# Top-k attention and dropless experts on one core: TensorE, ScalarE and VectorE put in a hand-written order by groups of rows

## The chip, the cores and the metric

The kernel runs on one core of one Trainium2 chip. The metric is device time in microseconds (us), the median of three runs. In the profile PE is TensorE's matmul, PEld its weight load, DVE VectorE, ACT ScalarE, POOL GpSimd and SP the engine that issues most of the DMAs.

## The reference

Two blocks follow each other. Attention has 8 batches, 8 heads, 576 rows, head size 64, and keeps the 32 largest scores of each row:

```
scores = scale * q @ k^T                       # 576 x 576 for each batch and head
kth    = 32nd largest score of each row
attn   = softmax(scores where scores >= kth)   # the rest is masked
x      = attn @ v, heads side by side          # 4608 x 512
logits = x @ w_gate                            # 8 experts
e      = argmax(logits);  gate = softmax(logits)[e]
out    = gate * (relu(x @ w1[e]) @ w2[e])      # w1 512 x 1024, w2 1024 x 512, all float32
```

## The kernel before

**Units, groups, tiles.** Two heads form a unit: 8 batches x 4 units. A unit has nine tiles of 128 rows (four for each head, and one that joins the last 64 rows of both). They are worked on in five groups: four pairs of tiles and a single one. So `work` has 160 groups, 20 for each batch. The loop over `work` (L673 to L710) runs, for group i:

- `search` (L241), on DVE: four rounds of MAX8 (L260) and MATCH_REPLACE8 (L268) over the halves' maxima, one MAX8 over the minima (L265), then `both` (L277) and the threshold `thr` (L281). In its last round it calls `between`, which is `fold` (L233: `hl`, a maximum and a minimum of the two halves of a score row, L237 and L238) for group i+1. On POOL it issues `nbias` (L262), `low` (L283) and `over` (L286).
- `transposed` (L313) for group i-1: for each tile four transposes on PE into a PSUM bank `wTm` (L321), the last 64 columns into `wTl` (L329), and copies to SBUF on ACT (L324 or L326, L332 or L334). Banks named `wTm`, `wTl`, `po`, `px`, `pl` and `rank` share two buffers (`bank`, L192).
- `scores` (L215) for group i+2: eight matmul instructions on PE (L225) into two PSUM tiles `sc` (two buffers), each copied by ACT to `s` (L230).
- `depths` (L291), ACT: `w = relu(low - STEEP * s)` (L295); `weights` (L301): POOL takes `s - w` (L305), ACT the exponential (L308), which also sums the row.
- After a unit's last group, `close` (L613): `outputs` (L336) makes the unit's product with the values on PE (`po`, L350), copies it (`oT`, L351), transposes it (`px`, `pl`, L354 and L357), takes the gate's logits (L360) and copies all of it to SBUF (L355, L364, L366); then the loads of the unit after next are issued on SP. `settle` (L628) follows in steps that `later` (L656) calls in the next groups: `divisors` (L368, DVE), `scaled` (L376, POOL), and after a batch's last unit `route` (L392) and `table` (L462), which choose an expert for each row and write the rows, sorted, to DRAM (`scatter`, L436, an indirect DMA on POOL).
- `pieces` (L594): the expert blocks. A block is 128 sorted rows of one expert: `turned` (L529, transposes `xtp`), 8 pieces of `ph` matmuls (L548), 8 pieces of `py` matmuls (L558), ReLU `hT` and scaling `y` on ACT (L553, L562), and a scatter of the result to `out` on POOL (L563). There are 16 pieces to a block and 40 blocks in the common path. 24 of them are spread over the groups; their number per batch is 0, 4, 4, 5, 4, 5, 4 for the rows of batches 0 to 6, with a new rate taken at the group `FIRST` = 5 of the next batch. Two (`KEEP`) cover the last batch's routing, and 14 (`ALWAYS`) run alone at the end.

**What sets the order.** Except where a dependency is written (`pinned`, L523, keeps an expert's matmul behind the newest score matmul or gate matmul; two `add_manual_dep` in `scaled`), the framework's scheduler orders each engine's queue by its own model of durations. Each engine executes its queue in that order, whatever is ready.

**After the blocks** two tests follow, each with its own branch: rows beyond the 14 blocks (L723), and an exact second pass where `doubt` says that the two-half search may have lost a value (L737). Neither branch is taken here.

Of the kernel before, what the change touches and what calls it, by code (L numbers as in the profile page):

```python
# [43 lines left out]
def kernel(  # L44
# [36 lines left out]
    nc = tc.nc  # L81
# [81 lines left out]
    rest_i = const.tile([1, 1], I32, name="rest_i")  # L163
    done = const.tile([1, E], F32, name="done")
# [13 lines left out]
    def open_pools(st, exact):  # L178
# [10 lines left out]
        k.last_pe = None  # L189
        k.top = 0  # L190

# [3 lines left out]
    def load_unit(b, u):  # L195
        n = SimpleNamespace(u=u)
        qkb = k.load.tile([P, 2, S], F32, name="qkb")
        nc.sync.dma_start(qkb, qk[b, u, :, :, :])
        n.q, n.k = qkb[:, 0, :], qkb[:, 1, :]
        n.v = k.load.tile([P, KC, P], F32, name="vb")  # L200
        nc.sync.dma_start(n.v, v[b, u, :, :].rearrange("(c p) d -> p c d", p=P))
        return n
# [12 lines left out]
    def scores(n, tiles):  # L215
# [6 lines left out]
        for j in range(2):  # L222
            for ps, h, rows, cols in todo:
                d = slice(h * D, (h + 1) * D)
                k.last_pe = nc.tensor.matmul(  # L225
                    ps[rows, j, 0:HF], n.q[d, cols], n.k[d, j * HF:(j + 1) * HF], start=True, stop=True
                ).ins
        s = k.att.tile([P, 2, 2, HF], F32, name="s", bufs=2 if k.exact else 3)
        for m, ps in enumerate(got):
            nc.scalar.copy(s[:, m, :, :], ps[:, :, 0:HF])  # L230
        return s
# [9 lines left out]
    def search(n, tiles, s, hl, between):  # L241
# [14 lines left out]
        for r in range(R):  # L256
# [4 lines left out]
            if r == 0:  # L261
                nc.gpsimd.tensor_scalar_mul(nbias[:, m2], tops[:, m2, 0], -scale)  # L262
                if not k.exact:
                    for m in m_all:
                        nc.vector.max(out=tops[:, m, TOP_K + 1:TOP_K + 9], in_=hl[:, 1, m, :])  # L265
            if r < R - 1:
# [16 lines left out]
        nc.gpsimd.tensor_scalar_mul(low[:, m2], thr[:, m2], STEEP)  # L283
        if not k.exact:
            c = 2 * tiles[0] if len(tiles) == 2 else 2 * NC
            nc.gpsimd.tensor_tensor(  # L286
                n.over[:, c:c + len(tiles)], tops[:, m2, TOP_K + 8], thr[:, m2], op=ALU.subtract
            )
        return low, nbias

    def depths(tiles, s, low):  # L291

        w = k.att.tile([P, 2, S], F32, name="w", bufs=3)
# [7 lines left out]
    def weights(n, tiles, s, w, nbias):  # L301

        c = 2 * tiles[0] if len(tiles) == 2 else 2 * NC
        for m in range(len(tiles)):
            k.last_pool = nc.gpsimd.tensor_tensor(  # L305
                w[:, m, :], s[:, m, :, :].rearrange("p j k -> p (j k)"), w[:, m, :], op=ALU.subtract
            ).ins
            nc.scalar.activation(  # L308
                w[:, m, :], w[:, m, :], AF.Exp, scale=scale, bias=nbias[:, m:m + 1],
                accum_out=n.z[:, c + m:c + m + 1],  # L310
            )
# [24 lines left out]
    def outputs(n, x):  # L336

        oT = oT_of[k.unit % 2]
        k.unit += 1
        for j in range(2):  # L340
            q = slice(j * HF, (j + 1) * HF)
            po = bank("po")
            for c in range(KC):
                for h in range(2):
# [5 lines left out]
                    nc.tensor.matmul(po[r, 0:HF], lhsT, rhs, start=(c == 0), stop=(c == KC - 1))  # L350
            nc.scalar.copy(oT[:, q], po[:, 0:HF])  # L351
# [3 lines left out]
        nc.scalar.copy(x[:, 0:NC, n.u * P:(n.u + 1) * P], px[:, :].rearrange("p (t d) -> p t d", t=NC))  # L355
        pl = bank("pl")
        k.last_pe = nc.tensor.transpose(pl[:, 0:P], oT[:, SM:], ident).ins  # L357
        lw = 2 * E
        for t in range(KC):
            k.last_pe = nc.tensor.matmul(  # L360
                pl[:, P + t * lw:P + (t + 1) * lw], oT[:, t * P:(t + 1) * P],
                wg2[:, n.u, :, :].rearrange("p h e -> p (h e)"), start=True, stop=True,
            ).ins
        nc.scalar.copy(x[:, NC, n.u * P:(n.u + 1) * P], pl[:, 0:P])  # L364
        n.lt = k.small.tile([P, KC, 2, E], F32, name="lt")
        nc.scalar.copy(n.lt, pl[:, P:P + KC * lw].rearrange("p (t h e) -> p t h e", t=KC, h=2))  # L366

# [8 lines left out]
    def scaled(n, x, lg):  # L376

        rzb = rz_of[n.u % 2][:, :].rearrange("p (t h) -> p t h", h=2)
        put = nc.gpsimd.tensor_tensor(n.lt, n.lt, _inner(rzb, E), op=ALU.mult).ins
        if not k.exact:  # L380
            tc.add_manual_dep(put, k.last_pool.name, AFTER)
        if n.u:
            nc.gpsimd.tensor_tensor(lg, lg, n.lt[:, :, 0, :], op=ALU.add)
            nc.gpsimd.tensor_tensor(lg, lg, n.lt[:, :, 1, :], op=ALU.add)
        else:
            nc.gpsimd.tensor_tensor(lg, n.lt[:, :, 0, :], n.lt[:, :, 1, :], op=ALU.add)
        xu = x[:, :, n.u * P:(n.u + 1) * P].rearrange("p t (h d) -> p t h d", h=2)
        put = nc.gpsimd.tensor_tensor(xu, xu, _inner(rzb, D), op=ALU.mult).ins
        if not k.exact:
            tc.add_manual_dep(put, k.last_pool.name, AFTER)  # L390

    def route(x, lg):  # L392
# [11 lines left out]
        nc.vector.tensor_tensor(lg, lg, _inner(mx[:, :], E), op=ALU.subtract)  # L404
        nc.scalar.activation(lg, lg, AF.Exp)
# [4 lines left out]
        nc.tensor.matmul(rp[:, 256:256 + KC * E], ones, ohf, start=True, stop=True)  # L410
        rk = k.small.tile([P, 2, KC * E], F32, name="rk")
# [24 lines left out]
        def scatter(i):  # L436
# [5 lines left out]
            if not k.exact:  # L442
                for other in mine:
# [18 lines left out]
    def table(n, last):  # L462
# [34 lines left out]
        slot_i = sm.tile([1, 2, NSLOT], I32, name="slot_i")  # L497
        nc.vector.tensor_copy(slot_i[:, :, 0:n], slot_f[:, :, 0:n])
        if last:
            nc.vector.tensor_copy(rest_i, upto[:, E - 1:E])  # L500
        else:
# [21 lines left out]
    def pinned(put):  # L523

        if k.last_pe is not None and not k.exact:
            tc.add_manual_dep(put.ins, k.last_pe.name, AFTER)
        return put

    def turned(n):  # L529

        ps = k.ps_m.tile([P, DT, P], F32, name="xtp", tag="m")
        for dt in range(DT):
            pinned(nc.tensor.transpose(ps[:, dt, :], n.x[:, 0, dt * P:(dt + 1) * P], ident))
# [3 lines left out]
    def block(n, following=lambda: None):  # L537
# [5 lines left out]
        for half in range(2):  # L543
            ph = k.ps_m.tile([P, FT // 2, P], F32, name="ph", tag="m")
            for f in range(FT // 2):
                fc = half * (FT // 2) + f
                for dt in range(DT):
                    pinned(nc.tensor.matmul(  # L548
                        ph[:, f, :], n.w1[:, 0, dt, fc * P:(fc + 1) * P], n.xT[:, dt, :],
                        start=(dt == 0), stop=(dt == DT - 1),  # L550
                    ))
                if f == FT // 2 - 1:
# [265 lines left out]
```

## Time and profile before

| | |
|---|---|
| median of 3 runs | 1660.99 us (1656.68 to 1665.58) |
| the profiled execution, its own time | 1664.02 us |
| its span in the trace | 1662.2 us |
| first `thr` (L281) starts | 19.06 us |
| 50th `thr` (group 10 of batch 2) | 421.67 us |
| 160th and last `thr` | 1381.44 us |
| last result scatter issued (L563) | 1648.85 us |

The span is cut by two times in this table. Up to the last `thr` DVE searches one group after the other, and the other engines serve it and fill in pieces of expert blocks; after it PE alone works, on the kept blocks and the 14 last ones. The second row of `thr` matters because up to there hardly any expert block runs. Page 1 of the profile gives busy shares over the whole span, so they mix these stretches; a table of busy time by stretch keeps them apart.

### The profile page before, as it was taken

Reading aid. Unit: us, or ns where it says so; the run is one execution under the profiler, and the core shown is the slowest. Engines: PE = TensorE matmul, PEld = TensorE weight load, DVE = VectorE, ACT = ScalarE, POOL = GpSimd, SP = SyncE. Lnnn points to the kernel's source line nnn. Section 1 sums busy time; section 2 is a strip of 40 time slices with the busy share of each in tenths; the row PEclk is TensorE's granted clock in tenths of the full one; section 3 lists DMA queues with packets and bytes.
Section 4 is the critical chain, followed back from the end, with each engine's and each line's share of the span. In section 5 each row is a group of like instructions: output and inputs, shape, how many; then the busy total and the mean of one; then the engine's idle time right before and its main releaser. Section 6 shows DMA issues by size and latency. Waiting matters only on the chain. (4 is left out here: it accounts for less than half of the span.)

```text
span 1662.2 us, 24985 instructions
## 1 busy us (share of the span) xinstructions
PE 1457.5 (88%) x7874; PEld 924.2 (56%) x7874; DVE 1237.7 (74%) x4258; ACT 934.2 (56%) x1937; POOL 666.3 (40%) x993
## 2 busy tenths in 40 slices
PE   5777878788999989898999999899999987899996
PEld 3444434445555555555666555556655554577764
DVE  8999979999899898889888999977889994000000
ACT  4666646665676676656665777656566763111111
POOL 3444544545444544444345544544345543000000
PEclk8666656668999999989999999989999988999998
DMA  1000010007232533245441633353334333788883
GB/s 59 23 23 23 34 40 23 23 23 266 82 142 78 208 142 120 91 159 202 171 151 54 241 137 136 113 189 136 137 128 160 136 115 143 285 308 304 295 319 130
DMA packets 102191, 230.69 MB, mean 139 GB/s; under 512 B 5150, under 2 KB 25630, under 8 KB 102048
## 3 DMA queue, kind: packets, MB, share of 16 engines
q1 hardware_dynamic: 95904, 210.06, 35.2%
q0 software_dynamic: 6144, 18.92, 3.1%
q8 instruction: 66, 1.08, 0.3%
q14 instruction: 77, 0.63, 0.1%
HBM read 207.68 MB, written 22.33 MB: 138 GB/s over the span
## 5 line engine op out<-in xcount | busy, mean ns | idle before, releaser
L305 POOL TENSOR_TENSOR w<-s,w 128x576 f32<-128x576 f32 x288 | 424.2, 1487 | 302.3 <-ACT w L295 301.8
L260 DVE MAX8 tops<-scr 128x8 f32<-128x288 f32 x864 | 353.8, 445 | 0.9
L225 PE MATMUL sc<-qkb 64*128 64x288 f32 (+1 forms) x1280 | 346.0, 506 | 7.3 <-DMA qkb<-in_qk_dram 5.9
L548 PEld LDWEIGHTS ph<-xTs,w 128*128 128x128 f32 x2560 | 305.3, 198 | 24.2 <-issue 21.9
L548 PE MATMUL ph<-xTs,w 128*128 128x128 f32 x2560 | 315.6, 283 | 1.3 <-ACT xTs L535 1.3
L558 PE MATMUL py<-w,hT 128*128 128x512 f32 x640 | 310.4, 629 | 5.4 <-ACT hT L553 5.3
L308 ACT ACTIVATE w<-w,nbias 128x576 f32<-128x576 f32 x288 | 223.3, 776 | 158.4 <-POOL w L305 156.9
L321 PE MATMUL wTm<-ident,w 128*128 128x128 f32 x1152 | 197.4, 312 | 115.7 <-ACT w L308 113.7
L295 ACT ACTIVATE w<-s,low 128x576 f32<-128x576 f32 x288 | 215.6, 776 | 98.4 <-POOL low L283 98.2
L321 PEld LDWEIGHTS wTm<-ident,w 128*128 128x128 f32 x1152 | 147.8, 158 | 200.5 <-ACT w L308 169.2
L268 DVE MATCH_REPLACE8 scr<-tops,scr 128x288 f32<-128x288 f32 x576 | 250.1, 440 | 0.0
L237 DVE TENSOR_TENSOR hl<-s 128x576 f32<-128x576 f32 (+1 forms) x160 | 130.1, 813 | 129.4 <-ACT s L230 129.0
L225 PEld LDWEIGHTS sc<-qkb 64*128 64x128 f32 (+1 forms) x1280 | 158.4, 204 | 102.6 <-issue 56.7
L558 PEld LDWEIGHTS py<-w,hT 128*128 128x128 f32 x640 | 121.9, 201 | 143.3 <-issue 133.8
L230 ACT COPY s<-sc 128x576 f32<-128x576 f32 x288 | 173.4, 636 | 34.6 <-PE sc L225 25.6
L324 ACT COPY wT<-wTm 128x512 f32<-128x512 f32 x256 | 140.5, 586 | 42.3 <-PE wTm L321 42.2
L350 PE MATMUL po<-wT,vb 128*64 128x288 f32 x1024 | 157.2, 455 | 1.4 <-ACT wT L326 1.4
L563 POOL DMA_INDIRECT out_dram<-y,xg x40 | 40.7, 1017 | 242.3 <-ACT y L562 220.4
L262 POOL TENSOR_SCALAR nbias<-tops 128x2 f32<-128x2 f32 (+1 forms) x160 | 34.9, 218 | 246.4 <-DVE thr L281 139.9
L238 DVE TENSOR_TENSOR hl<-s 128x576 f32<-128x576 f32 (+1 forms) x160 | 129.6, 810 | 0.0
L268 DVE MATCH_REPLACE8 scr<-tops,hl 128x288 f32<-128x288 f32 x288 | 125.3, 440 | 0.1
L260 DVE MAX8 tops<-hl 128x8 f32<-128x288 f32 x288 | 124.8, 441 | 0.0
(119 smaller groups left out, 1244.2 us busy)
## 6 DMA issues: line engine op xcount, KB each, us to landing
w<-in_moe_w_dram SPq DMA_DIRECT2D x80, 2048.0 KB, 11.2
qkb<-in_qk_dram SPq DMA_DIRECT2D x32, 576.0 KB, 3.9
xg<-x_rows SPq DMA_DIRECT2D x40, 257.0 KB, 2.7
vb<-in_v_dram SPq DMA_DIRECT2D x32, 320.0 KB, 3.2
x_rows<-blank SPq DMA_DIRECT2D x9, 257.0 KB, 4.5
x_rows<-x,posi POOLq DMA_INDIRECT x40, 3.0
out_dram<-y,xg POOLq DMA_INDIRECT x40, 2.8
wg<-in_moe_w_gate_dram SPq DMA_DIRECT2D x1, 16.0 KB, 1.9
```

Of the source, the lines that this page charges most:

```text
L225: k.last_pe = nc.tensor.matmul(ps[rows, j, 0:HF], n.q[d, cols], n.k[d, j * HF:(j + 1) * HF], start=True, stop=True).ins
L230: nc.scalar.copy(s[:, m, :, :], ps[:, :, 0:HF])
L260: nc.vector.max(out=tops[:, m, r * 8:(r + 1) * 8], in_=src[m])
L268: nc.vector.match_replace(out=scr[:, m, :], in_to_replace=tops[:, m, r * 8:(r + 1) * 8], in_values=src[m], imm_value=NEG,)
L295: nc.scalar.activation(w[:, m, :], s[:, m, :, :].rearrange("p j k -> p (j k)"), AF.Relu, scale=-STEEP, bias=low[:, m:m + 1],)
L305: k.last_pool = nc.gpsimd.tensor_tensor(w[:, m, :], s[:, m, :, :].rearrange("p j k -> p (j k)"), w[:, m, :], op=ALU.subtract).ins
L308: nc.scalar.activation(w[:, m, :], w[:, m, :], AF.Exp, scale=scale, bias=nbias[:, m:m + 1], accum_out=n.z[:, c + m:c + m + 1],)
L321: nc.tensor.transpose(pm[:, c * P:(c + 1) * P], w[:, m, c * P:(c + 1) * P], ident)
L324: nc.scalar.copy(n.wT[:, :, m, tiles[0] * P:(tiles[0] + 1) * P], pm4)
L350: nc.tensor.matmul(po[r, 0:HF], lhsT, rhs, start=(c == 0), stop=(c == KC - 1))
L548: pinned(nc.tensor.matmul(ph[:, f, :], n.w1[:, 0, dt, fc * P:(fc + 1) * P], n.xT[:, dt, :], start=(dt == 0), stop=(dt == DT - 1),))
L558: pinned(nc.tensor.matmul(py, hT[:, f, :], n.w2[:, 0, f, :], start=(f == 0), stop=(f == FT - 1)))
```

## The change

- **Order.** The loop stands in a `manual_schedule` for PE, ACT and DVE: on these engines the program's order is the queue's order. On POOL the small operations and L305 are put in program order too (`in_turn`), and the indirect DMAs behind the newest L305. `pinned` is gone. SP's order is still the scheduler's.
- **Score products ahead.** `scores` is split into `products` (PE) and copies (ACT). Products are issued four groups ahead, their copies three (`AHEAD`), and the copies stand between the exponentials: copy, exp, copy, exp. `s` has four buffers instead of three.
- **Place of each step.** For group i: search, depths, L305, transposes of group i-1, half of the pieces, copies and exponentials, products of group i+4, the other pieces.
- **Unit ends** run in named places over three groups: first group, both halves of `po` with the products between them and the first `oT` copy, no pieces; second, divisors, second `oT` copy, `px` and `pl`, their copies; third, `logits` and `rows` on POOL, after the first round of the search. A batch's routing follows in the next places, a step each.
- **Pieces** are handed out by tiles (`len(g)`), a group may catch up to four groups' worth, and a new rate starts at group 10 (`FIRST`), not 5.
- **End.** 6 of the 32 kept pieces run inside the last routing. The two tests at the end are put under one branch (`rare`).

```diff
-        s = k.att.tile([P, 2, 2, HF], F32, name="s", bufs=2 if k.exact else 3)
-        for m, ps in enumerate(got):
-            nc.scalar.copy(s[:, m, :, :], ps[:, :, 0:HF])
-        return s
+        return got
+
+    def scores(got):
+        s = k.att.tile([P, 2, 2, HF], F32, name="s", bufs=2 if k.exact else 4)
+        return s, [
+            lambda m=m, ps=ps: nc.scalar.copy(s[:, m, :, :], ps[:, :, 0:HF]) for m, ps in enumerate(got)
+        ]
...
+    def weights(n, tiles, w, nbias, beside=()):
         c = 2 * tiles[0] if len(tiles) == 2 else 2 * NC
+        for m in range(max(len(tiles), len(beside))):
+            for step in beside[m:m + 1]:
+                step()
+            if m < len(tiles):
+                nc.scalar.activation(
+                    w[:, m, :], w[:, m, :], AF.Exp, scale=scale, bias=nbias[:, m:m + 1],
+                    accum_out=n.z[:, c + m:c + m + 1],
+                )
...
-    FIRST = 5
-    ARRIVED = 9
+    FIRST = 10
+    ARRIVED = 10
+    AHEAD = 3
...
+        def ending(b, u):
...
+            next(out_steps)
+            yield "products"
+            next(out_steps)
+            if b * U + u + 2 < len(units):
+                load_values(unit[b * U + u + 2])
+            yield "weights"
+            next(out_steps)
+            yield "small"
+            divisors(n)
+            yield "turn"
+            next(out_steps)
+            yield "products"
+            next(out_steps)
+            yield "weights"
+            next(out_steps, None)
+            yield "begun"
+            logits(n, lg)
+            rows(n, x)
+            if u < U - 1:
+                return
+            yield "small"
+            steps = route(x, lg)
...
+                low, nbias = search(n, g, s_of[i], hl_of.pop(i), lambda: at_place("begun"), between)
+                at_place("small")
+                w_of[i] = depths(g, s_of[i], low)
+                less(g, s_of.pop(i), w_of[i])
+                scatter(1)
...
+                now = max(0, min(int(credit + 0.5), room))
+                at_place("turn")
+                if i:
+                    turn(i - 1)
+                if i and work[i - 1][2] == groups[-1]:
+                    late = ending(*work[i - 1][:2])
+                    place = next(late)
+                    now = 0
+                else:
+                    credit = min(credit - now, 4 * rate)
+                pieces(now // 2)
+                steps = []
+                if i + AHEAD < len(work):
+                    s_of[i + AHEAD], steps = scores(got_of.pop(i + AHEAD))
+                weights(n, g, w_of[i], nbias, steps)
+                if i + AHEAD + 1 < len(work):
+                    multiply(i + AHEAD + 1)
+                at_place("products")
+                at_place("weights")
+                pieces(now - now // 2)
...
+        with tc.manual_schedule(engines={mybir.EngineType.PE, mybir.EngineType.Activation, mybir.EngineType.DVE}):
+            loop()
```

## The prediction

> **What bounds the kernel now.** I read first the span in 40 slices, then the busy time by stretch, then the waits, then DVE's timeline.
>
> ```profile
> PE   5777878788999989898999999899999987899996
> DVE  8999979999899898889888999977889994000000
> PEclk8666656668999999989999999989999988999998
> ...
> 10.74:436.75 426.01, 339.26 (x1487) 191.75 (x1486) 396.51 (x1341) 270.46 (x564) 195.85 (x291) 0.70 0.14 48
> 436.75:1381.44 944.69, 864.98 (x4964) 551.86 (x4961) 831.44 (x2857) 616.54 (x1291) 443.82 (x655) 0.95 0.40 142
> 1428.00:1662.20 234.20, 213.05 (x1188) 151.58 (x1186) 0.00 (x0) 34.09 (x57) 14.66 (x15) 0.97 0.75 275
> ```
>
> The three long rows give a stretch, its length, then the busy time of PE, PEld, DVE, ACT and POOL, PE's granted clock, the DMA share and GB/s. In the first stretch (hardly any expert pieces) DVE is busy 396.51 of 426.01 us, 93%. In the second, with pieces, DVE is busy 88% and PE 92%: both are near full, and neither alone sets the end. In the third PE is alone; the change does not reach it, apart from its end.
>
> ```profile
> DVE hl L237 <- ACT s L230: 129.0, 54, 8.9
> PEld wTm L321 <- ACT w L308: 169.2, 112, 6.6
> ACT w L295 <- POOL low L283: 98.2, 54, 4.3
> ...
> 1363.12 1.30 DVE L237 TENSOR_TENSOR hl<-s 128x576 f32<-128x576 f32 x1 [3.42 <-ACT s L230]
> 1364.34 1.96 DVE L238 TENSOR_TENSOR hl<-s 128x576 f32<-128x576 f32 x1
> ...
> L237 DVE TENSOR_TENSOR hl<-s x160: 437/749/1884, 9.4 to 1372.8; 128x576 f32<-128x576 f32 x128, 128x288 f32<-128x288 f32 x32
> ...
> 1378.30 3.04 DVE L277 TENSOR_TENSOR both<-tops 128x9 f32<-128x9 f32 x1
> 1378.53 2.77 POOL L305 TENSOR_TENSOR w<-s,w 128x576 f32<-128x576 f32 x2
> ```
>
> DVE's one large idle time, 129.0 us in 54 waits, is the fold waiting for ACT's score copies. A second loss hides in its busy time: two-input operations of DVE stretch when POOL's L305 runs. The small `both`, usually 0.15 us, took 3.04 us beside a pair of L305; the fold's median is 749 ns, its longest 1884, and by the rows that keep shapes apart its pair means are 886 and 881 ns: (886 + 881 - 2 x 750) ns x 128 = 34 us.
>
> The sum is made on the profiled execution: 10.7 us to the first MAX8, searches up to the last `thr` at 1381.44, then 280.8 us of tail; 1662.2 in all. Its own time was 1664.0, and the median of the runs is 1661.0; I carry a difference of the span over to the median.
>
> **The searches alone.** DVE's starts in undisturbed pairs give 0.365 us for a MAX8 in a row of two, 0.42 for a MATCH_REPLACE8 with its load, 0.67 for one half of a fold. A pair is 10 x 0.365 + 6 x 0.42 + 2 x 0.67 = 7.51. Program order adds dependent steps that the scheduler had filled with the next group's MAX8: the last MAX8 to `both` takes 0.50 and `both` to `thr` 0.27 where the single tile ran alone (808.17, 808.67, 808.94 us), so 0.13 + 0.27 + 0.08 more: 7.99. A pair that folds the single group: 7.39. The single tile runs 0.54 + 0.50 us a round unfilled (1375.16 to 1378.30), 5.43 with its neighbour's fold. `divisors`: 0.75. A unit is 3 x 7.99 + 7.39 + 5.43 + 0.75 = 37.5 us. Routing and table, by the end of the last batch (about 1.5, 1.8 and 3.5 us), 6.8 a batch. The trace of before shows 39.2 us for a unit without pieces (125.58 to 164.77): the cost in order is small beside what the waits cost.
>
> **Copies three groups ahead (gain).** The fold waits only if ACT is over two groups behind DVE, some 15 us; the longest such wait is 8.9. So I take the 129.0 us out and put DVE's own order in. *Up to group 50*: before, 421.67. After, 10.7 + 10 x 37.5 + 2 x 6.8 = 400 (the first routings fall in here), a gain of 22. PE must follow at the clock of 0.70: one unit without pieces takes PE (rows below) 20 us at full clock, 29 at 0.70, under 37.5 even with 5 us of waits. The extreme that all of PE is at half clock, 40 us, would give 10 x 2.5 = 25 us back; I take none, since the rows show full-clock durations too (0.76 us for four score matmuls at 225.63, 1.33 at 236.81).
>
> **Transposes, pieces and copies in one order (decides).** From there 22 units with pieces, 959.8 us before, 43.6 each. PE's prices at full clock, start to start: transposes of a pair 0.97, `wTl` 0.35, scores 1.2, `po` 2 x 2.72, `px` and `pl` 2.1, a piece 0.92 (3.68 for 32 `ph`). A unit: 5 x 1.2 + 4 x 1.32 + 0.8 + 5.44 + 2.1 = 20; with one block 34.7.
> Now the waits that the written order adds. `wTl` takes the bank of the first `wTm`, so PE waits for its copy on ACT: pair done at 1.6 instead of 1.32. Half of the pieces (1.78 x 0.92): 3.2. The products need the copies of three groups ahead, which stand behind `wTt`, a copy and an exponential: 2.05 + 0.55 + 0.87 + 0.64 = 4.1, so PE goes on at 4.2, ends at 5.1, other pieces 6.75. `hT`, `y` and `xTs` (0.6 each) stand in ACT's queue where the pieces stand, and behind them the score copies, or the next `depths`; half of some 0.9 events a group cost about 1 us: 0.45. A pair: 7.2. By the same steps the unit's first group (no pieces) takes 0.5 + 1.0 + 2.72 + 1.2 + 2.72 = 8.1, the second (its own pieces and those put off) 1.6 + 3.2 + 1.2 + 2.1 + 3.2 + 0.45 = 11.8, the single one 6.1. Sum 8.1 + 11.8 + 2 x 7.2 + 6.1 = 40.4 with one block a unit; five blocks a batch add 4 x 0.92 = 3.7: 44.1. DVE's 37.5 + 1.7 = 39.2 lies below, so PE sets this stretch. The rates from group 10 on give 14 units of the first kind and 8 of the second: 14 x 40.4 + 8 x 44.1 = 918, against 959.8, a gain of 41. Bounds: PE without any added wait, limited by DVE or 38.4 with five blocks, 14 x 39.2 + 8 x 39.2 = 862 (gain 97); every one of the four ACT events of a block in front of the copies, at 0.6 plus a piece of wait, 6.1 us instead of 2.0 a unit: 1008 (loss 48). I stay at 918, since the events fall in either half of a group.
>
> **POOL and SP.** `low` is queued behind `logits` and `rows` (0.37 + 2 x 0.27 + 1.26 = 2.2 us), which wait for the copies of `px`; behind `low` waits ACT's `depths`. Once a unit, and ACT is busy with those copies until then; up to 2 us, inside the 0.45 terms. A result's scatter (1.02 us) stands behind L305 and waits for `y`; `low` of the next group can stand behind it, 24 times 1 us at most, counted in the range. On SP the score load leaves when the unit's last products are issued, five groups before use, against 3.9 us to land; the values likewise (3.2). The first weights of a batch need 2.7 + 11.2 us after the fifth scatter, at group 7 or 8 of the batch; pieces start at group 10, 15 us or more later: nothing. Were they late, PE's written order would hold everything for up to 11 us, six times.
>
> **The rule against it.** The trace shows both sides of a clash stretched by up to the other's whole length. The Trainium skill, page "SBUF — State Buffer", section "Who interferes with whom", says that a DVE instruction with two SBUF inputs contends with a GpSimd instruction that reads SBUF, and that whoever issues first holds the pair for its whole instruction. That speaks against an order that lets L305 slip: it runs 1.1 to 3.9 us after `thr`, and the next fold at 5.4, so an ACT that is 1.5 us late brings them together, which by the page alone could cost a pair of L305 in every group.
> By the rows, a full clash cost the pair at 1363.12 us 1.30 + 1.96 - 1.50 = 1.76 us. A DVE that is held by missing copies folds after the second copy, past L305, so I expect fewer clashes; a gain of the 34 us is in the 37.5 already.
>
> **The end.** The last scatter ends at 1649.8, lands about 2.8 us later, and 9.6 us remain, in which two branches stood; now one. No row prices a branch; bounds 0 and -9.6, I take -3. Six kept pieces move into the last routing: the same work, and 26 pieces, 24 us, still cover the scatters (6.4) and a load.
> Sum: -22 - 41 - 3 = -66: 1661 - 66 = 1595 us.
>
> **Rivals.** (1) PE's waits vanish and DVE sets every unit: -22 - 97 - 3: 1539. For: PE was 91% busy only by modelled ends. Against: two fullish engines in lockstep. (2) PE eats the gain: units with pieces stay at 43.6, early gain half, 1661 - 11 - 3 = 1647, and within 8 us of 1661 if they take 44 to 44.7. For: PE is 92% busy there already. (3) Slower: ACT's expert steps hold the score copies in the strict order (`hT` waits for PE, PE's products wait for the copies behind it). It decides from 44.6 us a unit, since 22 x 1.0 then equals the 25 us gained elsewhere; at the bound of 1008 it is 1661 + 48 - 25 = 1684. For: before, the scheduler could let copies pass; PE, ACT and POOL now share one chain. Against: ACT is busy 65% there. (4) That the order is not kept: the rows would repeat and the time stay.
>
> **Numbers.** Forecast 0.50, rival 1 0.16, rival 2 0.10 (0.06 of it within the bound), rival 3 0.22, rival 4 0.02 (same). I call 8.3 us, 0.5%, the bound of what can be told from no change. Faster 0.50 + 0.16 + 0.04 = 0.70, same 0.08, slower 0.22. The forecast's own range is 1560 to 1640; the range of 8 in 10 runs from inside rival 1, 1545, to inside rival 3, 1678.
>
> **What would show it.** The fold's waits on ACT near zero up to group 50, and that `thr` near 400 us; undisturbed pairs of 8.0 us; PE idle before `wTl` and before the products; the last `thr` near 1318; fold durations near 750 ns. I am wrong if pairs with pieces take over 8 us while PE waits for score copies, or if L305 meets the fold in most groups.

## The result, and the profile after

The changed kernel takes 1715.9 us (median of 4 runs, 1713.22 to 1716.63) against 1661.4 us (4 runs, 1656.68 to 1665.58) for the kernel before in the same comparison: ratio 1.0326 with an interval of 1.0296 to 1.0356, 55 us slower. The forecast was 1595 us and the range ended at 1678. The profiled execution took 1716.52 us, with a span of 1714.6.

Lines are those of the changed kernel now: the fold is L250 and L251, `both` L291, `thr` L295, `low` L297, L305 of before is L318, the score copy L243, `depths` L309, `logits` and `rows` L405 to L416, the routing's first step `mx` L421, the result scatter L585.

The span in 40 slices, from the page of the changed kernel:

```profile
PE   5788777867898899879987899889888889699996
DVE  7999999989998899889968999889869992000000
PEclk8666677666999899989998999899999999899998
```

The two 6 in DVE's row did not stand there before: in these slices DVE, busy at 9 in most others, waits. The same kernel by stretch (columns: stretch, length, busy time of PE, PEld, DVE, ACT, POOL, granted clock, DMA share, GB/s); the cuts are the 50th `thr`, the last `thr`, and the first of the 14 last blocks:

```profile
10.70:421.97 411.27, 314.06 (x1349) 175.91 (x1347) 396.81 (x1287) 257.45 (x543) 186.66 (x282) 0.68 0.10 32
421.97:1417.84 995.87, 852.63 (x5045) 552.90 (x5043) 898.01 (x2910) 617.34 (x1298) 455.36 (x660) 0.95 0.39 140
1417.84:1480.00 62.16, 44.29 (x282) 31.80 (x282) 8.97 (x51) 16.18 (x37) 13.65 (x17) 0.91 0.53 187
1480.00:1714.60 234.60, 214.48 (x1192) 152.77 (x1192) 0.00 (x0) 34.72 (x57) 14.68 (x15) 0.97 0.76 277
```

Before, the same four stretches took 410.97, 959.77, 44.86 and 235.90 us (cuts at 421.67, 1381.44, 1426.30). So nothing was gained up to group 50, 36.1 us were lost in the 22 units with pieces, 17.3 between the last `thr` and the last blocks, and 1.3 gained behind: 0.3 + 36.1 + 17.3 - 1.3 = 52.4, the difference of the two spans. DVE's waits over the whole span:

```profile
DVE mx L421 <- POOL lg L408: 54.5, 8, 13.4
DVE hl L250 <- ACT s L243: 40.6, 21, 5.8
```

The fold's wait for score copies fell from 129.0 us (54 waits) to 40.6 (21). In its place DVE waits 54.5 us in 8 waits, one for each batch, for the gate's logits from POOL (20.0 before).

**Where in a batch it went.** The table is worked from the starts of `thr`: a unit's time runs from the last `thr` of the unit before to its own last. The 22 units with pieces are those from the third unit of batch 2 on. "Plain" is the mean of the 12 that are third or fourth in their batch. In the first and second units of a batch the previous batch is routed; what these two take beyond two plain units is "added by routing", the mean of 5 batches. All columns but the last are read from one profiled run of each kernel. The rows of the experiments belong to the next section.

| kernel | 50th `thr` | last `thr` | plain unit | added by routing | median us |
|---|---|---|---|---|---|
| before | 421.7 | 1381.4 | 42.3 | 5.8 | 1661.4 |
| changed | 422.0 | 1417.8 | 41.6 | 16.3 | 1715.9 |
| e4: 26 blocks left out | 419.2 | 1330.4 | 38.7 | 11.9 | 1608.1 (one run) |
| e1: DVE free | 413.5 | 1387.7 | 41.7 | 11.6 | 1686.8 |
| e7: logits behind `low` | 415.5 | 1396.3 | 41.7 | 12.8 | 1692.7 |
| e14: e1 and e7 together | 394.0 | 1322.0 | 39.0 | 14.2 | 1619.1 |
| e13: e7, block ended early | 415.8 | 1396.3 | 41.7 | 12.7 | 1684.1 |
| e10: e14, block ended early | 392.6 | 1318.1 | 39.0 | 13.7 | 1608.8 |
| e11: only DVE written | 443.7 | 1396.9 | 39.2 | 18.2 | 1676.8 |
| e12: no written order | 414.0 | 1344.8 | 39.4 | 12.8 | 1637.1 |
| e15: e12 and e7 | 412.9 | 1324.2 | 38.8 | 11.5 | 1617.6 |
| e8: before, copies three ahead | 427.2 | 1355.4 | 40.0 | 9.8 | 1642.8 |

The plain units are a little faster than before: 22 x (41.57 - 42.31) = -16.3 us. The routing costs more: 5 x (16.26 - 5.79) = +52.4. The sum is the 36.1 lost.

**One routing, read line by line.** The changed kernel's timeline, all engines (start, duration, engine, line, operation; in brackets the idle time before it and what ended it):

```profile
896.53 0.23 ACT L390 COPY lt<-pl 128x80 f32<-128x80 f32 x1 [4.15 <-PE pl L384]
...
899.43 0.59 PE L581 MATMUL py<-w,hT 128*128 128x512 f32 x1
...
900.06 0.69 ACT L584 ACTIVATE y<-py,xg 128x512 f32<-128x512 f32 x1 [2.65 <-PE py L581]
...
901.02 1.04 POOL L585 DMA_INDIRECT out_dram<-y,xg  x1 [13.56 <-ACT y L584]
902.10 0.24 POOL L275 TENSOR_SCALAR nbias<-tops 128x2 f32<-128x2 f32 x1
902.29 0.32 POOL L405 TENSOR_TENSOR lt<-lt,rz 128x80 f32<-128x80 f32 x1
...
903.04 0.27 POOL L408 TENSOR_TENSOR lg<-lg,lt 128x40 f32<-128x40 f32 x1
903.26 1.26 POOL L416 TENSOR_TENSOR x<-x,rz 128x640 f32<-128x640 f32 x1
903.34 0.20 DVE L421 TENSOR_REDUCE mx<-lg 128x5 f32<-128x40 f32 x1 [13.44 <-POOL lg L408]
...
904.49 0.21 POOL L297 TENSOR_SCALAR low<-thr 128x2 f32<-128x2 f32 x1
...
904.74 0.77 ACT L309 ACTIVATE w<-s,low 128x576 f32<-128x576 f32 x1 [3.99 <-POOL low L297]
```

DVE had its threshold at 889.73; its next written instruction is `mx`, and it stands idle for 13.44 us. `mx` waits for the logits (L408), these stand on POOL behind a result scatter (L585), the scatter waits 13.56 us for `y` on ACT, and `y` for the block's last `py` on PE. All the while `low` of the threshold that was ready at 889.73 waits in POOL's queue, until 904.49, and ACT's `depths` behind it. Nothing here is slow; each queue is held in turn by its first instruction. The scatter is not the whole of it: the logits' own input, `lt`, was copied by ACT (L390) only at 896.53, since `px` and `pl` stand behind pieces and score products in PE's order. POOL could have begun at 896.75 and began at 902.29 (L405): of the 13.44 us the scatter accounts for some 5.5, PE's order for the rest. In the other three batches with pieces `mx` waits 3.55 us each, with the scatter out of the way.

### The profile page after: what moved, and what is told of

It reads as the page before. It is cut to its first block, busy times and chain, and to the rows that moved or that the text cites. A ratio compares the mean times of both kernels' runs of the same rounds, so it can differ in the third digit from the quotient of the medians.

```text
span 1714.6 us, 24871 instructions
## 1 busy us (share of the span) xinstructions
PE 1429.6 (83%) x7874; PEld 916.1 (53%) x7874; DVE 1306.2 (76%) x4261; ACT 928.1 (54%) x1937; POOL 672.6 (39%) x993
## 5 line engine op out<-in xcount | busy, mean ns | idle before, releaser
L318 POOL TENSOR_TENSOR w<-s,w 128x576 f32<-128x576 f32 x288 | 412.2, 1450 | 264.9 <-ACT w L309 264.1
L234 PE MATMUL sc<-qkb 64*128 64x288 f32 (+1 forms) x1280 | 344.4, 514 | 70.9 <-ACT s L243 61.7
L581 PE MATMUL py<-w,hT 128*128 128x512 f32 x640 | 319.3, 629 | 8.9 <-ACT hT L577 8.7
L309 ACT ACTIVATE w<-s,low 128x576 f32<-128x576 f32 x288 | 209.3, 770 | 180.7 <-POOL low L297 179.7
L234 PEld LDWEIGHTS sc<-qkb 64*128 64x128 f32 (+1 forms) x1280 | 172.3, 210 | 223.5 <-ACT s L243 173.6
L342 PE MATMUL wTm<-ident,w 128*128 128x128 f32 x1152 | 187.2, 309 | 10.5 <-ACT x L391 7.3
L243 ACT COPY s<-sc 128x576 f32<-128x576 f32 x288 | 181.4, 631 | 9.8 <-PE sc L234 9.8
L581 PEld LDWEIGHTS py<-w,hT 128*128 128x128 f32 x640 | 115.2, 197 | 126.7 <-issue 111.3
L585 POOL DMA_INDIRECT out_dram<-y,xg x40 | 46.0, 1150 | 345.5 <-ACT y L584 323.3
L250 DVE TENSOR_TENSOR hl<-s 128x576 f32<-128x576 f32 (+1 forms) x160 | 134.0, 837 | 40.6 <-ACT s L243 40.6
L350 PE MATMUL wTl<-ident,w 128*64 128x128 f32 x288 | 70.7, 323 | 111.8 <-ACT wT L345 111.6
L297 POOL TENSOR_SCALAR low<-thr 128x2 f32<-128x2 f32 (+1 forms) x160 | 36.5, 228 | 254.8 <-DVE thr L295 219.4
L372 PEld LDWEIGHTS po<-wT,vb 128*64 128x64 f32 x1024 | 74.3, 150 | 95.6 <-ACT wT L347 35.2
## 6 DMA issues: line engine op xcount, KB each, us to landing
w<-in_moe_w_dram SPq DMA_DIRECT2D x80, 2048.0 KB, 12.4
```

The lines of the kernel that those rows point to most:

```text
L234: nc.tensor.matmul(ps[rows, j, 0:HF], n.q[d, cols], n.k[d, j * HF:(j + 1) * HF], start=True, stop=True)
L243: lambda m=m, ps=ps: nc.scalar.copy(s[:, m, :, :], ps[:, :, 0:HF]) for m, ps in enumerate(got)
L309: nc.scalar.activation(w[:, m, :], s[:, m, :, :].rearrange("p j k -> p (j k)"), AF.Relu, scale=-STEEP, bias=low[:, m:m + 1],)
L318: k.last_pool = in_turn(nc.gpsimd.tensor_tensor(w[:, m, :], s[:, m, :, :].rearrange("p j k -> p (j k)"), w[:, m, :], op=ALU.subtract)).ins
L342: nc.tensor.transpose(pm[:, c * P:(c + 1) * P], w[:, m, c * P:(c + 1) * P], ident)
L372: nc.tensor.matmul(po[j][r, 0:HF], lhsT, rhs, start=(c == 0), stop=(c == KC - 1))
```

## The experiments

Each result is set against runs of the kernel before on the same chip (medians of 1657.6 to 1662.9 us). The first four take the loss apart by engine.

**e1: DVE left to the scheduler.**

```diff
-manual_schedule(engines={PE, Activation, DVE})
+manual_schedule(engines={PE, Activation})
```

> VectorE is left to the scheduler, TensorE and ScalarE keep the written order. Theory A (VectorE's written order is what costs: a pair of tiles takes 7.98 us in it and 7.45 to 7.66 us in the scheduler's, the routing stands in one piece): VectorE's busy time falls by 40 to 60 us, and the time from 1716 to 1660 to 1680. Theory B (waits behind the result scatter on GpSimd): within 10 us of 1716, with the routing's long waits unchanged. Theory C (the written order of TensorE and ScalarE holds everything): VectorE's saving turns into waits for score copies and the time stays above 1700.

1686.8 us, ratio 1.0188 (1.0149 to 1.0227). DVE's written order costs some 29 us by itself, about half of the loss.

**e7: the logits and rows put behind the subtraction (L318) of their group**, so that `low` no longer stands behind them; the routing follows one group later.

```diff
-search(..., lambda: at_place("begun"), between)
+search(..., lambda: None, between)
 ...
 less(g, s_of.pop(i), w_of[i])
+at_place("begun")
```

> On GpSimd, logits and rows come behind the group's subtraction instead of ahead of low, and so a batch's routing starts one group later. Theory B2 (low stands behind logits and rows, which wait for ScalarE's copies, and VectorE's routing waits for the logits): the waits before the routing's first instruction (41 us up to the last threshold) fall under 10 us and the time to 1670 to 1690. Theory A alone (VectorE's order): the waits were idle time that other work would fill; under 10 us.

1692.7 us, ratio 1.0182 (1.0128 to 1.0237). The logits' place on POOL costs 23 us by itself. The edit does two things at once, and this run does not part them: `low` goes first, and the routing starts a group later, when its logits are mostly there (`mx` waits 33.2 us in 3 waits instead of 54.5 in 8). The gain lies up to group 50 and in the units that route; a plain unit stays at 41.7 us.

**e4: no pieces among the groups.** 26 of the 40 blocks (all but the last 14) are left out, so its time, of a single run, is short by their work.

> No expert block runs before the last batch's routing (24 of 40 blocks are left out, so their rows are not computed); searches, routing and tables stay. Only the time of the last threshold is of interest, 1417.8 us with the blocks. Theory A (VectorE's order): still 1300 to 1330 us, since eight batches then take 160 to 165 us each as the first two do. Theory C (TensorE and ScalarE late because of the pieces): the same; the difference to 1418, about 100 us, is what pieces cost in this order. If the last threshold came at 1260 or below, the written VectorE order would not matter.

The stretch up to its last `thr`, and DVE's waits:

```profile
10.70:1330.38 1319.68, 1004.69 (x4424) 564.70 (x4422) 1273.21 (x4195) 830.17 (x1758) 609.42 (x922) 0.68 0.09 28
```

```profile
DVE mx L421 <- POOL lg L408: 22.3, 8, 12.3
DVE hl L250 <- ACT s L243: 5.2, 1, 5.2
```

With no expert piece on PE, DVE is busy 1273.21 of 1319.68 us, and the last `thr` still comes at 1330.4, though PE's granted clock is 0.68 in this stretch (0.95 in the changed kernel's stretch with pieces). By the forecast's own figures DVE alone would have ended at 400 + 22 x 39.2 = 1262. A plain unit takes 38.7 us, and routing adds 11.9. Pieces then add 87 us in the changed kernel.

**e14: e1 and e7 together** (both edits above).

> VectorE left to the scheduler and the gate's logits and rows put behind GpSimd's subtraction; the kept block is not ended early. Theory B (the two mends help each other: with VectorE free the routing's steps are filled with searches, and with GpSimd unblocked these searches find their thresholds' partners ready): 1609 + 7 = 1616, last threshold near 1318 as in the best kernel. Theory A (they add up): 1716 - 29 - 23 = 1664, last threshold near 1368.

1619.1 us (1614.73 to 1628.34), ratio 0.975 (0.9706 to 0.9795): faster than before. Alone the two edits gave 29 and 23 us, together 97. The units say why: with either one alone a plain unit stays at 41.7 us, with both it takes 39.0. In the stretch with pieces, e1, e7 and e14, one fence each:

```profile
413.50:1387.70 974.20, 842.79 (x5035) 548.20 (x5035) 884.73 (x2905) 619.48 (x1300) 470.32 (x657) 0.96 0.39 142
```

```profile
415.48:1396.32 980.84, 844.77 (x5085) 544.78 (x5084) 904.27 (x2910) 622.04 (x1309) 463.37 (x664) 0.96 0.40 144
```

```profile
394.00:1321.97 927.97, 828.27 (x5063) 535.88 (x5063) 876.81 (x2905) 617.86 (x1301) 460.57 (x660) 0.99 0.42 151
```

From e7 to e14 DVE is busy 27 us less (the third busy time of the rows: 904.27 to 876.81) and idle 25 us less. From e1 to e14 its busy time changes by 8 us and its idle time by 38 (89.5 to 51.2), and nearly all of that is the fold's wait for score copies; DVE's waits in that stretch, e1 and then e14:

```profile
DVE hl L250 <- ACT s L243: 62.4, 24, 6.5
```

```profile
DVE hl L250 <- ACT s L243: 25.5, 10, 5.8
```

So with DVE free and POOL's queue unmended, DVE only reaches the next late copy sooner; with POOL mended and DVE written, its dependent steps hold it. Part of what makes the copies late can be read in e1's timeline. PE waits for the rows of a new batch's first block before their transposes (`xtp`), and ACT's copy `xTs`, the score copies and the fold stand behind:

```profile
580.91 1.11 PE L557 MATMUL xtp<-ident,xg 128*128 128x128 f32 x4 [6.11 <-DMA xg<-x_rows]
582.06 0.59 ACT L559 COPY xTs<-xtp 128x512 f32<-128x512 f32 x1 [6.63 <-PE xtp L557]
582.54 0.65 ACT L243 COPY s<-sc 128x576 f32<-128x576 f32 x1
583.84 0.64 ACT L243 COPY s<-sc 128x576 f32<-128x576 f32 x1
584.51 0.76 DVE L250 TENSOR_TENSOR hl<-s 128x576 f32<-128x576 f32 x1 [4.04 <-ACT s L243]
```

PE waits for these rows 23.3 us in e1's stretch with pieces and 23.1 in the changed kernel's, in five waits each, one a batch, and not at all in e7, e14 and before. Three of e1's fold waits stand right behind them, 14.7 of the 62.4 us (the one shown, and those that end at 760.34 and 1122.84). What makes the rest of its copies late is not traced here.

**e13: e7 with the kept block ended early (e9 below), DVE's order kept.**

> The changed kernel with the gate's logits and the rows put behind GpSimd's subtraction and the kept block ended before the last transposes; VectorE's hand-written order stays. Theory A (the costs add up, and what made the best kernel fast beyond their sum is chance): 1716 - 23 - 7 = 1686. Theory B (VectorE's written order is a floor of about 1330 us for the last threshold with no piece of an expert block, so mending GpSimd's queue cannot bring the last threshold under about 1380): 1675 to 1690, last threshold 1385 to 1397, VectorE's waits for the batch routing's maximum 20 to 35 us. Theory C (GpSimd's queue alone made the loss and VectorE's order costs nothing): under 1640.

1684.05 us, ratio 1.0134 (1.0087 to 1.018), last `thr` at 1396.3: the written order on DVE does not get under 1396 with POOL's queue mended, while e10, which differs from e13 only in that DVE is free, ends at 1318. With POOL mended and PE and ACT written, the written DVE order costs 75 us. (The time alone would also be the plain sum of the two gains, 1686; it is e14 that rules the plain sum out.)

**e11: only DVE written, PE and ACT left to the scheduler.**

> Only VectorE keeps the written order; TensorE and ScalarE are left to the scheduler. Theory A (VectorE's order sets the time): at least the 1330 us of the run without blocks up to the last threshold, and about 1375 to 1400 with them; 1670 to 1700. Theory C (TensorE's and ScalarE's written order costs most): 1650 to 1670.

1676.8 us, ratio 1.0094 (1.006 to 1.0129). The fold's waits are gone (5.6 us), yet the last `thr` stands at 1396.9, routing adds 18.2 us, and `mx` waits 49.8 us in 5 waits. DVE's order alone makes the kernel some 15 us slower than before, and 40 slower than e12 below. But freeing PE and ACT brings 39 us against the changed kernel, more than e1 or e7, and takes a plain unit to 39.2 us with DVE written and POOL unmended: the written order of PE and ACT has its part in the 41.6.

**e12: no written order on any engine**, with the copies three ahead and the new places of the program.

> The changed program with no engine in written order: copies three ahead, unit ends spread, pieces by tiles, one branch; the scheduler orders TensorE, ScalarE and VectorE. If the written order is the whole loss, this is as fast as the kernel before with copies three ahead or faster: 1625 to 1655. If the spread of the unit ends or GpSimd's program order costs too, 1665 to 1700.

1637.1 us, ratio 0.9862 (0.9829 to 0.9895). The rest of the change is a gain of 23 us; writing the three orders by hand costs 79.

**e15: e12 and e7.**

> No hand-written order at all, with the gate's logits and rows put behind GpSimd's subtraction. Theory D (the written order of TensorE and ScalarE is worth something once VectorE is free): 1625 to 1640, clearly above the 1609 of the best kernel. Rival (that order is worth nothing; the gain is GpSimd's queue and copies three groups ahead): 1605 to 1618.

1617.6 us (1616.29 to 1627.85), ratio 0.9757 (0.9703 to 0.9811), the same as e14's 1619.1. With POOL mended and DVE free, the written order of PE and ACT is worth nothing in the sum. By stretch it is: it brings 18.9 us up to group 50 (394.0 against 412.9) and loses 16.7 behind it (928.0 against 911.3).

**e8: the kernel before with the copies three ahead** and four `s` buffers, all else as it was.

```diff
-name="s", bufs=2 if k.exact else 3
+name="s", bufs=2 if k.exact else 4
-    s_of[i + 2] = ready(i + 2)
+    s_of[i + 3] = ready(i + 3)
```

> The kernel before, with one part of the change alone: score products and copies three groups ahead instead of two and four buffers, in the scheduler's order. If the fold's 123 us of waits come from copies that are issued too late, they fall by half or more and the time to 1590 to 1630. If they come from the order in which ScalarE and TensorE serve everything (a copy behind waits for TensorE), depth alone does little: 1645 to 1665.

1642.8 us (1635.12 to 1650.36), ratio 0.9897 (0.9831 to 0.9964). The fold's waits fall to 64.9 us. This one part of the change is a gain by itself, of some 17 us, though its size is uncertain: the four runs lie at 1635 to 1636 and 1649 to 1650. The place is certain: in the profiled run the 50th `thr` comes 5.5 us later than before, and the units with pieces take 31.5 less.

**e5: the result's scatter put later**, behind the next group's subtraction or ahead of the next block's transposes, to take it away from in front of the logits. A first form (e2), with the scatter only behind the subtraction, put instructions into a circle of waits and has no time.

> Each result scatter on GpSimd is issued behind the next group's subtraction (or ahead of the next block's transposes), when its input is done. Theory B (the scatter at the head of GpSimd's queue holds logits and low): the two waits of 13.4 us before the routing go, and some score-copy waits: 1685 to 1700. Theory D (the routing's wait is for TensorE's px and pl and ScalarE's copies, the scatter only stands in the same place): under 8 us.

1759.7 us, ratio 1.0585 (1.0529 to 1.0641): 44 us worse than the changed kernel, against what was expected. Two lines of its waits say why:

```profile
PE xtp L562 <- DMA xg<-x_rows: 100.3, 21, 15.1
DVE hl L255 <- ACT s L248: 81.9, 16, 7.5
```

The scatter reads the row numbers that lie in `xg`, so a later scatter frees `xg` later, the next block's rows are loaded late, and PE waits for them in its fixed order (41.2 us in 10 waits in the changed kernel). Yet it does settle the scatter's share of `mx`'s waits. In the stretch with pieces, changed kernel and e5, one fence each:

```profile
DVE mx L421 <- POOL lg L408: 37.5, 5, 13.4
```

```profile
DVE mx L426 <- POOL lg L413: 27.3, 5, 7.9
```

The two waits of 13.44 us become 7.9 each, the other three stay (3.5 to 4.0). So the scatter itself held 5.6 us, twice; the rest is the way of `px`, `pl` and `lt` through PE and ACT, as the expectation's theory D has it.

**The end.** Between the last `thr` and the first of the 14 blocks the changed kernel lost 17.3 us. Its timeline:

```profile
1432.11 0.60 PE L342 MATMUL wTm<-ident,w 128*128 128x128 f32 x4
...
1441.76 0.71 ACT L584 ACTIVATE y<-py,xg 128x512 f32<-128x512 f32 x1
1442.76 1.06 POOL L585 DMA_INDIRECT out_dram<-y,xg  x1 [15.06 <-ACT y L584]
1445.68 0.34 SPq L543 DMA_DIRECT2D xg<-x_rows  x1
...
1464.18 8.79 SPq L485 DMA_DIRECT2D x_rows<-blank  x8
...
1477.11 0.35 SPq L543 DMA_DIRECT2D xg<-x_rows  x1
...
1479.91 0.87 PE L557 MATMUL xtp<-ident,xg 128*128 128x128 f32 x3 [15.35 <-DMA xg<-x_rows]
```

The last transposes come 14.3 us after the last `thr` (4.3 before), since PE's written order has the products and pieces of groups before in front of them. The first row scatter of the last batch is issued at 1451.14, 33.3 us after the last `thr` (1403.20, 21.8, before): 11.5 us. The blank rows, 13.0 us behind that scatter instead of 9.2, add 3.9; from them to the load of the first block's rows it is 12.9 instead of 11.2, since the eight blank loads take 8.79 us to issue instead of 5.47: 1.8. Sum 17.2. The blank rows wait for the row scatters to land, and these land late. The five scatters' time from issue to landing, changed kernel and before:

```profile
DMA to landing us min/median/max: 7.4/8.5/9.2
```

```profile
DMA to landing us min/median/max: 2.7/3.4/3.4
```

The last one lands at 1463.86, and the first blank row is issued at 1464.18. When these scatters were issued a block's weight loads, issued at 1446.26 and 1446.87, were still on their way; the second landed only at 1465.5, 18.6 us after its issue. Before, the weights had landed (1393.96) before the first scatter (1403.20). That the loads slow the scatters fits this and was not tested alone. Three kernels tried to mend the 17 us.

*e9*: the block that PE has finished is ended (`y`, its scatter, the next loads) before the last transposes, not when the next piece is asked for.

```diff
+if next(current, "end") == "end":
+    current = None
 ...
 turn(len(work) - 1)
```

> Ahead of the last transposes, the block whose last piece has run is ended (its scaling y and its result scatter are issued there, not when the next piece is asked for). Theory F (the scaling waits for the next piece, so the next block's loads start 9 to 12 us late, and the loads of blank rows and of the first of the 14 blocks stand behind them on SP): TensorE's wait of 15.4 us before that block falls to 8 to 11 us and the time by 4 to 8 us, to 1708 to 1712. If the row scatters alone set that wait, it stays within 2 us.

1708.6 us, ratio 1.0288 (1.0262 to 1.0314): 7 us less, and PE waits 9.54 us for the first block's rows instead of 15.35. A part of the 17 us was this late end: the loads stand 9.5 us sooner (1436.17), and the blank rows 8.0 us behind the first scatter, not 13.0.

*e6*: no pieces in the last two groups.

> No pieces in the last two groups; the same number of pieces in the ten groups before. Theory E (at the end, pieces stand in front of the last transposes in TensorE's written order, 10 us of the 17 us that the last routing comes later): the stretch from the last threshold to the first of the 14 blocks, 62 us, shrinks by 8 to 12 us and the time falls to 1704 to 1708. If TensorE's pieces are only moved and delay the earlier groups, the last threshold comes later by as much and the time stays.

1714.8 us, ratio 1.0303 (1.0241 to 1.0365): no change that its runs (1706.21 to 1717.47) can show. The last transposes are 3.3 us earlier (1428.79), not the 8 to 12 expected, the first row scatter 2.0 (1449.13) and the first of the 14 blocks 2.4 (1477.55); the wait for its rows stays (15.00 us), since PE ends the kept pieces earlier too. So late transposes do push the end back, but quiet groups moved them little.

*e3*: three blocks kept for the end, not two.

> Three blocks instead of two are kept for the end. If VectorE sets the time up to the last threshold, the block taken out of the loop costs nothing there and covers TensorE's 15.4 us wait before the 14 last blocks: 12 to 16 us less, about 1702, with the last threshold within 5 us of 1418. If TensorE sets that part, the last threshold also comes up to 15 us earlier and the time falls by about the same; only the place of the gain differs. If the wait is not for cover but for the chain of routing, it stays and the time too.

1723.1 us, ratio 1.0412 (1.0383 to 1.0442): 7 us worse than the changed kernel. One line of POOL's timeline holds the reason:

```profile
1455.68 0.97 POOL L466 DMA_INDIRECT x_rows<-x,posi  x1 [5.69 <-DMA xg<-x_rows]
```

The third block loads its rows from `x_rows` before the last batch's rows are written there, so the row scatters wait for that load.

**e10: the fastest version**, e14 and e9 together.

> Three edits together: VectorE left to the scheduler, logits and rows behind the subtraction, the last block ended early. If the three losses are separate (29, 23 and some 5 us), 1655 to 1665, the kernel before. If they are the same waits seen twice, 1675 to 1690.

1608.8 us (1605.01 to 1609.99), ratio 0.9687 (0.966 to 0.9714): 3.1% faster than before and 6.2% faster than the changed kernel (1608.8 / 1715.9 = 0.938). DVE's busy row on its page:

```profile
DVE  8999999999999999999898999999889981000000
```

and its stretches up to the 50th and the last `thr`:

```profile
10.70:392.60 381.90, 303.12 (x1348) 170.89 (x1346) 381.32 (x1292) 257.05 (x543) 193.60 (x281) 0.74 0.09 30
392.60:1318.06 925.46, 826.61 (x5063) 534.71 (x5063) 876.31 (x2906) 618.24 (x1301) 464.35 (x660) 0.99 0.42 151
```

Up to group 50 DVE is idle for 0.6 us. Behind, it is still idle for 49 us of 925, with pieces.

## Why the prediction was wrong, point by point

Between the forecast's 1595 and the 1715.9 us lie 121 us: 22 up to group 50, 77 in the 22 units with pieces (41 to be gained, 36 lost), 19 behind the last `thr` (3 to be gained, 16 lost), and the rest in how spans and medians differ.

**"Program order adds dependent steps": right for pairs, too small for the rest.** Undisturbed pairs take 7.98 to 7.99 us, as priced. The pair that folds the single group was priced at 7.39, and the single one at 5.43; in the seven early units without a routing they took 8.5 and 6.4 on the mean. Together that is the 2.1 us that such a unit takes more (39.6 against 37.5), 15 us in all; the two early units with a routing were priced at 44.3 and took 45.9 and 50.9, 8 more. So the gain of 22 us up to group 50 was used up. The 400 us expected there came, at 394.0 and 392.6, in e14 and e10, in which DVE is free, POOL mended, and PE and ACT still written; with these two free as well (e15) it is 412.9.

**Routing and table, "6.8 a batch": the first step that failed.** DVE works 2.2 us on `route`'s first part (530.71 to 532.92 us) and 8.4 without a search between on the rest (540.25 to 548.62): 10.6. These are some 40 small operations that each wait for the one before. The worse fault is in the sum: the 22 units with pieces were priced at 40.4 and 44.1 with no routing in them, as if it lay under PE's 2.5 us of slack a unit. It lies in one piece in one unit; with pieces it adds 16.3 us a batch: by the trace 10.6 of DVE's own steps and 7.5 of waiting for the logits on the mean, less what else such a unit saves. 918 us were forecast and 995.9 came: the plain units fit (22 x 41.6 = 915), and the difference of 78 is the 5 x 16.3 = 81 of routing.

**"PE sets this stretch": wrong, though its number looked right.** The plain units were forecast at 41.7 (918 / 22) and took 41.6. PE's waits that the sum named exist and are long (in the changed kernel `wTl` waits 111.6 us for its copy, the score products 61.7 for theirs). But e14 has PE's and ACT's written order as it was, and its plain units take 39.0: these waits are no floor. They are not without effect either, since e11, with PE and ACT free and the rest as in the changed kernel, comes to 39.2. So no one engine sets the 41.6; it falls when PE and ACT are freed, or when DVE is freed and POOL mended together, and that 41.7 was forecast is luck. Rival 1's 39.2 is no match for e14's 39.0: it has 1.7 of routing in it, and a plain unit by it is 37.5. That e10's last `thr` stands at 1318, the forecast's own mark, is luck too, the sum of other terms.

**"POOL: up to 2 us, inside the 0.45 terms", "24 times 1 us at most": the second step that failed.** The order was seen: `low` behind the logits, the logits behind the copies of `px`, a scatter that waits for `y`. Each was priced by its own duration, and the chain by none. `mx` waited 13.4 us twice with pieces (until 903.34 and 1274.06) and 54.5 us in all. Of each 13.4 the scatter, which itself waits 13.56, held 5.6; the rest the logits waited for `px` and `pl`, far back in PE's order; and `low` stood on POOL behind both, with ACT behind it. What the logits' place ahead of `low` costs is 23 us with DVE written and 68 (1686.8 - 1619.1) with DVE free.

**"Pieces start at group 10, 15 us or more later: nothing": a term that came.** The written order asks for a new batch's rows sooner than its own pieces: a block's `following` puts the next block's transposes (`xtp`) in its middle, and the last block of the batch before reaches them one or two groups ahead of group 10. PE waits for the rows 2.5 to 6.1 us there, once a batch, 23.1 us in five waits (none before), and holds ACT and the score copies, as e1's lines show. In e7 and e14 these waits are gone; what they cost alone no run shows.

**The rivals.** The result is on rival 3's side, slower, and 32 us beyond its bound (1684), but not in the main by its mechanism: ACT's score copies behind expert steps would show as a fold that waits, and the fold's waits fell to a third; that some of what is left stands behind `xTs` is its share. That the order is not kept is out.

**"Copies three groups ahead (gain)": right in kind.** 129.0 us of waits became 40.6, and in the kernel before alone the step brings 17 us (e8). Of the gain of 34 us by fewer clashes with L318 some 14 came. The pair folds by shape, in the changed kernel:

```profile
L250 DVE TENSOR_TENSOR hl<-s 128x576 f32<-128x576 f32 x128 | 111.1, 868 | 40.6 <-ACT s L243 40.6
L251 DVE TENSOR_TENSOR hl<-s 128x576 f32<-128x576 f32 x128 | 100.8, 788 | 0.0
```

(868 + 788 - 2 x 750) ns x 128 = 20 us are still stretched, against 34 before, and 26 us in e10, the fastest. The Trainium skill, page "SBUF — State Buffer", section "Who interferes with whom", has DVE instructions with two SBUF inputs contend with GpSimd's reads; the stretched folds agree, but the fastest kernel has more of it than the changed one, so here it decides little.

**"The end, I take -3".** With one branch less, the time from the last scatter's end to the span's end went from 12.4 to 11.7 us. No run shows that the branch is the reason: in the experiments that run all 40 blocks it lies between 9.9 and 12.1 us with one branch, and at 12.0 in e8 with two. The 17.3 us in front were not foreseen: "the same work" is right, but its order put the last batch's row scatters 11.5 us later.

**What stays open.** What makes the rest of the score copies late when DVE is free and the logits stand in front of `low` (e1); how e7's gain divides between `low` going first, the later routing and the transposes that no longer wait for rows; what `px` and `pl` further ahead in PE's order would bring; why eight blank loads take 8.79 us to issue in one kernel and 5.47 in another.

## What to carry to other kernels

When an engine's order is written by hand, price every chain of small dependent steps as a block that stops the engine where it stands, in the very unit where it stands, and for each queue ask of every instruction that waits for another engine what stands behind it; a scatter that waits for its data can cost up to its wait, not its duration, so far as what stands behind it was ready (here 5.6 of 13.6 us). Try two suspects together as well as one by one: here DVE's order and POOL's, each mended alone, left the plain unit at 41.7 us, and both together took it to 39.0. On the engine that bounds the kernel a written order must fill the gaps behind dependent steps at least as well as the scheduler did; here it did not.

## What the runs showed of the hardware that was not expected

- Short DVE instructions that depend on each other take some 0.2 us each start to start (544.80 to 548.62 us in the changed kernel: 21 of `table`'s steps, 3.8 us), for one row of a few numbers; a MAX8 over 128 rows of 288 takes 0.365 start to start in a pair (532.92 to 533.65 us for two). The chain of 3.8 us costs about half of a pair's search.
- Eight 257 KB loads of blank rows took 8.79 us to issue on SP where the row load and two weight loads had been issued 17 us before, and 5.47 us in the kernel before and in e9, where these were issued 31 and 21 us before.
- Five row scatters issued while a block's weight loads were on their way took 7.4 to 9.2 us to land (from 1451.14 us on); in the kernel before, with the weights landed, 2.7 to 3.4.
